# FAVOR attention and a feed-forward block on one core: the attention products of a chunk as one step of eight heads

## The chip, the cores and the metric

The kernel runs on one core of one Trainium2 chip. A core has a matrix engine (TensorE, PE in the profile), VectorE (DVE), ScalarE (ACT), GpSimd (POOL) and SyncE (SP), whose queue here issues the transfers. The engines run their own instruction queues in order and wait for one another by semaphores. The metric is the device time of one execution in microseconds (us), lower is better.

## The reference

Linear attention with positive random features, then a layer norm and a feed-forward block (FFN) with a residual. Batch 8, 8 heads, 576 positions, head width 64, 128 features, model width 512, hidden width 2048.

```python
q_s, k_s = q * scale, k * scale              # scale = 64 ** -0.25
def phi(x):                                  # omega: 128 x 64
    proj = einsum('bhsd,md->bhsm', x, omega)
    h = proj - sum(x * x, -1, keepdims) / 2
    h = h - max(h, -1, keepdims)             # over the 128 features
    return exp(h) / sqrt(128)
q_p, k_p = phi(q_s), phi(k_s)
kv = einsum('bhsm,bhsd->bhmd', k_p, v)
z = sum(k_p, axis=2)
num = einsum('bhsm,bhmd->bhsd', q_p, kv)
den = einsum('bhsm,bhm->bhs', q_p, z)[..., None] + 1e-06
x = (num / den)  as  (8, 576, 512)           # heads side by side
xn = (x - mean) / sqrt(var + 1e-06) * g_ln   # over the 512
out = x + relu(xn @ w_ch1) @ w_ch2
```

## The kernel before, in words

**Tiles.** The 8 x 576 = 4608 tokens are cut into 36 chunks of 128; four chunks make a token tile of 512 (nine tiles, 0 to 8), two chunks a block (18). A chunk can straddle two batches (chunks 4, 13, 22 and 31), and then has its products in two row parts.

**Attention.** The keys of a batch are projected (L510), their row maximum taken (L442, DVE), exponentiated (L448, ACT) and summed with the values into kv (L480), which holds 65 columns a head: 64 of numerator and one of denominator. For a block's queries a transfer (qD) is split into two parts (L573 on ACT, L575 on DVE), projected with two matmuls (L582, L583, a feature pair), copied out of its bank (L230 on ACT), its maximum over the 128 partitions taken by an all-reduce on POOL (L604), subtracted on DVE (L607) and exponentiated (L610, ACT). The names wide0 to wide13 are 14 buffers that all these share.

**A chunk's product** is `gen_x`, the place of the change. PE multiplies query features with kv, one matmul a head and row part (L671), into PSUM banks of four heads each; DVE adds epsilon to the denominators (L678), inverts them (L680) and multiplies (L682) into x; then the layer norm's statistics (L698, L700). `gen_rs` makes the reciprocal root for a block of two chunks at once (L711, ACT at L713 and L715, then L717 to L723 on DVE), so it needs both chunks' statistics. `gen_xnT` normalises a chunk (L741, DVE); PE transposes it (L755, four to a chunk), ACT casts it out of the bank (L759) and DVE makes the low part of the split (L761), both into xnT, the transposed tile.

**FFN.** A token tile has 16 hidden slices. A slice of the first layer (`mm1`, L782 to L784) is 12 matmuls, of three split products for each of four weight parts; its relu is split by ACT and DVE (L793, L795); the second layer (`mm2`, L815 to L817) adds it to four accumulators with 12 matmuls. After the last slice `result` adds x (L826, DVE) and sends the chunk out (L829). The first layer's first slice of the next tile comes behind the second layer's last slice of this one. There is one xnT buffer: the transposes of the next tile can start only when the tile's last first-layer slice is issued, and the first slice needs all four chunks of it.

**What sets the order.** Every step is a Python generator, and a planner runs them all before the kernel exists: a step asks for an engine with an estimated cost, waits for a named event, or gets buffers, and the planner always issues the step that can start first by its estimates, by rank among equals. The FFN's rank is the last, so it fills in where attention has nothing ready. The outcome is one fixed order on each engine. A `get` of one bank is met as soon as any one of its banks is free; a `get` with a count is met only at a moment at which so many are free, and whoever asks for one takes them meanwhile:

```python
count = part.want[2] if len(part.want) > 2 else 1
free = sorted((n for n in what if n in self.places), key=self.places.get)[:count]
if len(free) == count:
```

PSUM has eight banks, b0 to b7. Until the FFN starts, attention has them all; from then on it has b0 and b1 (`at_now()`) for projections, key sums, products and transposes, the first layer b2 and b3, the accumulators b4 to b7. Until the start PE is kept busy with dummy matmuls on b7 (`warm`, L308, called spins here).

Of the kernel before, what the change touches and what calls it, by code (L numbers as in the profile page):

```python
# [17 lines left out]
ALU = mybir.AluOpType  # L18
AX = mybir.AxisListType
PE, ACT, DVE, POOL, SP = "PE", "ACT", "DVE", "POOL", "SP"  # L20
PSUM = bass.MemoryType.PSUM

P = 128
B, H, S, D = 8, 8, 576, 64
M = 128
# [8 lines left out]
EPS = 1e-6  # L34
# [34 lines left out]
class Plan:  # L69
# [73 lines left out]
    def free(self, *names):  # L143
        for n in names:
            assert n not in self.places, n
            self.places[n] = self.cur.seen()
            self.cur.holds -= n[0] == "b" and 0 < self.cur.holds
            self.wake(lambda w: w[0] == "get" and n in w[1])

    def done(self, key):  # L150
        self.made[key] = self.cur.seen()
        self.wake(lambda w: w == ("wait", key))
# [38 lines left out]
def favor_ffn(ctx, tc, kT, kTr, vF, vR, qT, qD, omT, gT, w1, w2, out):  # L191
# [12 lines left out]
    nc = tc.nc  # L204
# [5 lines left out]
    plan = Plan()  # L210
    free, done = plan.free, plan.done
# [7 lines left out]
    def dve(n, k=1, c=0.065):  # L219
        return "run", {DVE: k * (c + 0.00105 * n)}  # L220

    def us(eng, t):
        return "run", {eng: t}
# [16 lines left out]
    def wait(*key):  # L240
        return "wait", key
# [4 lines left out]
    def tile_of(tag, shape, dtype=F32, pool=None):  # L246
        pool = pool or (wp if tag[1].isdigit() and tag[0] == "w" else small if tag[0:2] in ("kv", "mb", "st") or tag[0] == "v" else sb)
        return pool.tile(shape, dtype, tag=tag, name=tag, bufs=1)
# [6 lines left out]
    def bank(tag, n=512):  # L255
        return tile_of(tag, [P, 512], F32, ps)[:, 0:n]
# [10 lines left out]
    mlp_on = []  # L267

    def at_now():
        return b_at if mlp_on else banks  # L270
# [34 lines left out]
    def warm(n):  # L305
        if not mlp_on:
            for _ in range(n):
                nc.tensor.matmul(pw, spin[:, 0:P], spin, start=True, stop=True)  # L308
# [80 lines left out]
    kvs, phis, xs, xnTs, pvs, pvt = {}, {}, {}, {}, {}, {}  # L389
# [27 lines left out]
    def kv_last(b):  # L417
        return kv_key(b, NFULL if b % 2 == 0 else NFULL - 1)
# [195 lines left out]
    def phi(blk, h, cols):  # L614
        p, o = h // 2, h % 2
        s, i = (o, p % 2) if TILED else (p % 2, o)
        return phis[blk, p // 2, s][1][:, i, cols]
# [10 lines left out]
    def gen_block(blk, b_turn):  # L628
        rank = plan.cur.rank
        for j in range(2):  # L630
            if blk < T // QB:
                plan.add(rank, gen_q(blk, j))
            else:
                for s in range(2):
                    plan.add(rank, gen_q2(blk, j, s))
        t_st = yield "get", n_st
        st = tile_of(t_st, [P, 64])
        for i in range(2):
            plan.add(rank + 6 + 2 * i, gen_x(2 * blk + i, t_st, st))
        plan.add(rank + 8, gen_rs(blk, t_st, st))  # L640
        for j in range(2):
            for s in range(2):
                yield wait("phi", blk, j, s)
        yield wait("num", 2 * blk)
        yield wait("num", 2 * blk + 1)
        free(*(phis[blk, j, s][0] for j in range(2) for s in range(2)), b_turn)


    def gen_x(c, t_st, st):
        blk, cols = c // 2, (c % 2) * P  # L650
        ends = sorted({0, P, *(b * S - c * P for b in range(B) if 0 < b * S - c * P < P)})
        parts = [(a, z, (c * P + a) // S) for a, z in zip(ends, ends[1:])]
        for j in range(2):
            for s in range(2):
                yield wait("phi", blk, j, s)
        for _, _, b in parts:
            for s in range(2):
                yield wait(*kv_last(b), s)
        t_x = yield "get", n_x
        x = tile_of(t_x, [P, DM])  # L660
        o = 16 * (c % 2)
        rank = plan.cur.rank

        def half(s):
            t_b = yield "get", at_now()
            yield us(PE, 0.9 * len(parts) if mlp_on else 1.13)
            pn = bank(t_b)[:, 0 : 4 * (D + 1)].rearrange("p (a b) -> p a b", b=D + 1)
            for i in range(4):
                h = 4 * s + i
                for a, z, b in parts:  # L670
                    nc.tensor.matmul(  # L671
                        pn[a:z, i], phi(blk, h, slice(cols + a, cols + z)), kvs[b][1][:, h], start=True, stop=True
                    )
                warm(i % 2)
            done(("nummm", c, s))
            dn = st[:, o + 4 * s : o + 4 * s + 4]
            yield us(DVE, 0.13)
            nc.vector.tensor_scalar(out=dn, in0=pn[:, :, D], scalar1=EPS * M, scalar2=None, op0=ALU.add)  # L678
            yield us(DVE, 0.1)
            nc.vector.reciprocal(dn, dn)  # L680
            yield dve(4 * D, 1, 0.12)
            nc.vector.tensor_tensor(  # L682
                out=x[:, 4 * s * D : 4 * (s + 1) * D].rearrange("p (a b) -> p a b", b=D),
                in0=pn[:, :, 0:D],
                in1=dn.rearrange("p (a b) -> p a b", b=1).to_broadcast([P, 4, D]),
                op=ALU.mult,
            )
            free(t_b)
            done(("x", c, s))

        plan.add(rank, half(0))
        yield from half(1)
        yield wait("nummm", c, 0)
        done(("num", c))
        yield wait("x", c, 0)
        bn, mv = st[:, o + 8 : o + 14], st[:, 32 + 2 * (c % 2) : 34 + 2 * (c % 2)]
        yield dve(DM)
        nc.vector.bn_stats(bn, x)  # L698
        yield us(DVE, 0.1)
        nc.vector.bn_aggr(mv, bn)  # L700
        xs[c] = t_x, x, mv[:, 0:1], st[:, 38 + c % 2 : 39 + c % 2]
        done(("mv", c))
# [224 lines left out]
```

## Time and profile before

| | us |
|---|---|
| median of three runs | 1043.08 |
| lowest, highest | 1042.95, 1043.17 |
| the profiled execution | 1042.56 |
| its span | 1040.8 |
| PE busy | 1032.0 |
| DVE busy | 498.3 |
| ACT busy | 357.1 |
| POOL busy | 133.5 |
| first FFN matmul | 49.07 |

The profile is of one execution. Its rows give the start or the sum of busy time, the mean length of one instruction in ns where a group is shown, and the idle time of the engine just before, with the instruction that ended it. The granted clock of TensorE is 1.0 in the whole run. L12 is line 12 of the kernel before; from L664 on, the lines of the changed kernel have smaller numbers: its product is L670, the reciprocal L682, the statistics of a block L707 to L719, the normalisation L737, the transposes L751, the subtract into xnT L757, the FFN L778 to L780 and L811 to L813, the results L822.

### The profile page before, as it was taken

How to read it: one execution, taken by the hardware profiler on the slowest of the kernel's cores; microseconds unless marked ns; L12 is line 12 of the kernel's file. 1: busy time of each engine (PE TensorE's matmuls, PEld its weight loads, DVE VectorE, ACT ScalarE, POOL GpSimd, SP SyncE). 2: the span in 40 equal slices, each digit the busy share in tenths (PEclk: the TensorE clock that was granted, in tenths of full speed). 3: DMA queues.
4: the chain of work that ended last, by engine and by line, in shares of the span. 5: the costliest groups of instructions: out<-in, count | busy, mean ns of one | idle time of the engine just before them, and what ended most of it. 6: DMA issues, size and time to landing. Idle time of an engine off the chain costs nothing.

```text
span 1040.8 us, 14483 instructions
## 1 busy us (share of the span) xinstructions
PE 1032.0 (99%) x5778; PEld 863.4 (83%) x5778; DVE 498.3 (48%) x1045; ACT 357.1 (34%) x810; POOL 133.5 (13%) x80
## 2 busy tenths in 40 slices
PE   9999999999999999999999999999999999999998
PEld 7888888888887888888887888888878888888886
DVE  6999878366347521663147422751274134113112
ACT  7699746335334421253025421241133111102100
POOL 6000424014002300050002200140022000000000
PEclk9999999999999999999999999999999999999999
DMA  9564222121213100420032100200030010001001
GB/s 358 213 195 150 82 82 91 62 72 51 73 43 130 42 11 1 143 61 1 1 99 85 41 1 1 102 21 1 1 122 1 0 41 1 1 1 42 1 1 41
DMA packets 30308, 64.08 MB, mean 62 GB/s; under 512 B 3488, under 2 KB 3616, under 8 KB 30240
## 3 DMA queue, kind: packets, MB, share of 16 engines
q1 hardware_dynamic: 30240, 63.14, 17.9%
q8 instruction: 46, 0.75, 0.3%
q14 instruction: 22, 0.18, 0.1%
HBM read 53.69 MB, written 9.44 MB: 61 GB/s over the span
## 4 chain that ended last, share of the span: by engine, by line
PE 93%; DVE 4%; DMA 2%; SPq 1%; issue 1%; ACT 0%; ACTq 0%
PE b L815 13%; PE b L782 13%; PE b L784 12%; PE b L817 12%; PE b L816 12%; PE b L783 12%; PE b L480 5%; PE b L671 5%; PE b L510 3%; PE b L582 1%; PE b L583 1%; PE b L755 1%; DMA w<-w 1%; DVE x L826 1%; DMA w<-vF 0%
## 5 line engine op out<-in xcount | busy, mean ns | idle before, releaser
L795 DVE SCALAR_TENSOR_TENSOR hid<-b,hid 128x512 fp32r<-128x512 f32 x144 | 99.3, 689 | 382.5 <-ACT hid L793 381.9
L793 ACT ACTIVATE hid<-b 128x512 fp32r<-128x512 f32 x144 | 86.3, 599 | 445.8 <-PE b L784 445.4
L815 PE MATMUL b<-w,hid 128*128 128x512 f32 x576 | 231.6, 402 | 0.0
L782 PE MATMUL b<-xnT,w 128*128 128x512 f32 x576 | 230.4, 400 | 0.0
L817 PE MATMUL b<-w,hid 128*128 128x512 f32 x576 | 225.2, 391 | 0.0
L784 PE MATMUL b<-xnT,w 128*128 128x512 f32 x576 | 225.0, 391 | 0.1
L816 PE MATMUL b<-w,hid 128*128 128x512 f32 x576 | 224.9, 390 | 0.0
L783 PE MATMUL b<-xnT,w 128*128 128x512 f32 x576 | 224.5, 390 | 0.0
L604 POOL PARTITION_ALL_REDUCE wide<-wide x72 | 132.4, 1877 | 658.2 <-ACT st L713 268.3
L784 PEld LDWEIGHTS b<-xnT,w 128*128 128x128 f32 x576 | 108.2, 188 | 23.6 <-DVE xnT L761 0.5
L817 PEld LDWEIGHTS b<-w,hid 128*128 128x128 f32 x576 | 108.2, 188 | 23.0
L815 PEld LDWEIGHTS b<-w,hid 128*128 128x128 f32 x576 | 108.4, 188 | 22.6
L782 PEld LDWEIGHTS b<-xnT,w 128*128 128x128 f32 x576 | 108.4, 188 | 21.8
L783 PEld LDWEIGHTS b<-xnT,w 128*128 128x128 f32 x576 | 108.4, 188 | 20.6
L816 PEld LDWEIGHTS b<-w,hid 128*128 128x128 f32 x576 | 108.5, 188 | 20.3
L448 ACT ACTIVATE kp<-b,mb 128x128 f32<-128x128 f32 x272 | 75.3, 388 | 51.4 <-DVE mb L442 51.4
L671 PEld LDWEIGHTS b<-kv,wide 128*128 128x128 f32 (+1 forms) x640 | 67.2, 181 | 6.9 <-issue 2.8
L607 DVE TENSOR_TENSOR wide<-wide,wide 128x512 f32<-128x512 f32 x72 | 65.1, 909 | 13.3 <-POOL wide L604 12.8
L480 PEld LDWEIGHTS b<-v,kp 128*128 128x128 f32 (+1 forms) x576 | 64.2, 191 | 6.5 <-issue 1.6
L671 PE MATMUL b<-kv,wide 128*128 128x65 f32 (+1 forms) x640 | 66.8, 261 | 2.3 <-DVE st L678 1.2
L480 PE MATMUL b<-v,kp 128*128 128x65 f32 (+1 forms) x576 | 64.0, 272 | 0.0
L442 DVE TENSOR_REDUCE mb<-b 128x4 f32<-128x512 f32 x72 | 46.6, 681 | 30.9 <-PE b L510 30.8
(71 smaller groups left out, 800.0 us busy)
## 6 DMA issues: line engine op xcount, KB each, us to landing
w<-w SPq DMA_DIRECT2D x32, 512.0 KB, 8.9
wide<-qD SPq DMA_DIRECT2D x64, 256.0 KB, 2.7
out<-x SPq DMA_DIRECT2D x36, 256.0 KB, 2.0
v<-vF SPq DMA_DIRECT2D x28, 260.0 KB, 2.9
wide<-kT SPq DMA_DIRECT2D x28, 256.0 KB, 2.7
w<-vF SPq DMA_DIRECT2D x4, 260.0 KB, 4.8
v<-vR SPq DMA_DIRECT2D x4, 260.0 KB, 4.0
w<-kT SPq DMA_DIRECT2D x4, 256.0 KB, 4.8
```

Of the source, the lines that this page charges most:

```text
L448: nc.scalar.activation(out=kp[:, j], in_=pk[:, i], func=AF.Exp, scale=1.0, bias=mb[:, j : j + 1])
L480: nc.tensor.matmul(o[:, i], kp[r, slot(h)], v[r, h], start=(n > 0 or c + i == 0), stop=(n > 0 or (c == NFULL and i == 3)),)
L604: nc.gpsimd.partition_all_reduce(mx, qc, P, bass_isa.ReduceOp.max)
L671: nc.tensor.matmul(pn[a:z, i], phi(blk, h, slice(cols + a, cols + z)), kvs[b][1][:, h], start=True, stop=True)
L782: nc.tensor.matmul(ph, w[:, 0, cs], xnT[:, 0, k], start=(k == 0), stop=False)
L783: nc.tensor.matmul(ph, w[:, 1, cs], xnT[:, 0, k], start=False, stop=False)
L784: nc.tensor.matmul(ph, w[:, 0, cs], xnT[:, 1, k], start=False, stop=(k == NK - 1))
L793: nc.scalar.activation(out=hl[:, 0], in_=ph, func=AF.Relu)
L795: nc.vector.scalar_tensor_tensor(out=hl[:, 1], in0=ph, scalar=0.0, in1=f32(hl[:, 0]), op0=ALU.max, op1=ALU.subtract)
L815: nc.tensor.matmul(accs[i], hl[:, 0, cs], w[:, 0], start=(f == 0), stop=False)
L816: nc.tensor.matmul(accs[i], hl[:, 0, cs], w[:, 1], start=False, stop=False)
L817: nc.tensor.matmul(accs[i], hl[:, 1, cs], w[:, 0], start=False, stop=(f == NF - 1))
```

## The change

Before, a chunk's product was two generators, one for four heads each; each got one bank, and had its own epsilon, reciprocal and multiplication. Now one step gets two banks at once, issues the matmuls of all eight heads, adds epsilon in two instructions (one for each bank), takes one reciprocal of 128x8 over both, and multiplies in two instructions, after each of which its bank is free. The planner's estimates are the sums of the former ones; the reciprocal's estimate is paid once. The event that says that a chunk's matmuls are issued (`num`) comes now with the step itself.

```diff
-        def half(s):
-            t_b = yield "get", at_now()
-            yield us(PE, 0.9 * len(parts) if mlp_on else 1.13)
-            pn = bank(t_b)[:, 0 : 4 * (D + 1)].rearrange("p (a b) -> p a b", b=D + 1)
-            for i in range(4):
-                h = 4 * s + i
-                for a, z, b in parts:
-                    nc.tensor.matmul(
-                        pn[a:z, i], phi(blk, h, slice(cols + a, cols + z)), kvs[b][1][:, h], start=True, stop=True
-                    )
-                warm(i % 2)
-            done(("nummm", c, s))
-            dn = st[:, o + 4 * s : o + 4 * s + 4]
+        t_b = yield "get", at_now(), 2
+        yield us(PE, 1.8 * len(parts) if mlp_on else 2.26)
+        pn = [bank(t)[:, 0 : 4 * (D + 1)].rearrange("p (a b) -> p a b", b=D + 1) for t in t_b]
+        for h in range(H):
+            for a, z, b in parts:
+                nc.tensor.matmul(
+                    pn[h // 4][a:z, h % 4], phi(blk, h, slice(cols + a, cols + z)), kvs[b][1][:, h], start=True, stop=True
+                )
+            warm(h % 2)
+        done(("num", c))
+        dn = st[:, o : o + H]
+        for s in range(2):
             yield us(DVE, 0.13)
-            nc.vector.tensor_scalar(out=dn, in0=pn[:, :, D], scalar1=EPS * M, scalar2=None, op0=ALU.add)
-            yield us(DVE, 0.1)
-            nc.vector.reciprocal(dn, dn)
+            nc.vector.tensor_scalar(
+                out=dn[:, 4 * s : 4 * s + 4], in0=pn[s][:, :, D], scalar1=EPS * M, scalar2=None, op0=ALU.add
+            )
+        yield us(DVE, 0.1)
+        nc.vector.reciprocal(dn, dn)
+        for s in range(2):
             yield dve(4 * D, 1, 0.12)
             nc.vector.tensor_tensor(
...
-            free(t_b)
-            done(("x", c, s))
-
-        plan.add(rank, half(0))
-        yield from half(1)
-        yield wait("nummm", c, 0)
-        done(("num", c))
-        yield wait("x", c, 0)
+            free(t_b[s])
```

Since the planner sets the order, the change moves far more rows than it edits. Three places follow. In the rows, the left of the arrow is what is written, then what is read; b0 to b7 are banks, x6 and x7 the chunks 6 and 7, st3 the small statistics of their block; the number after an underscore only tells one use of a buffer from another.

PE, the product of chunk 7 in tile 0. Before, its two halves (b0_1706, then b1_1728) are six second-layer matmuls apart, and the next feature pairs (om_hi, om_lo) come behind:

```order
L671 MATMUL b0_1706<-kv1_95,wide5_1583 128x65
...
L815 MATMUL b4_783<-w2_120_1341,hid0_1587 128x512
...
L671 MATMUL b1_1728<-kv1_95,wide11_1489 128x65
...
L815 MATMUL b6_798<-w2_120_1341,hid0_1587 128x512
...
L582 MATMUL b0_1764<-wide4_1680,om_hi_82 128x512
...
L582 MATMUL b1_1776<-wide3_1684,om_hi_82 128x512
```

Now, with 12 first-layer matmuls of slices w1_120 to w1_150 and six second-layer ones between the product of chunk 6 and these rows:

```order
L582 MATMUL b1_1754<-wide4_1680,om_hi_82 128x512
L583 MATMUL b1_1754<-wide4_1680,om_lo_83 128x512
L582 MATMUL b0_1759<-wide3_1687,om_hi_82 128x512
L583 MATMUL b0_1759<-wide3_1687,om_lo_83 128x512
L811 MATMUL b6_795<-w2_130_1373,hid1_1658 128x512
...
L811 MATMUL b7_802<-w2_130_1373,hid1_1658 128x512
...
L670 MATMUL b1_1776<-kv1_95,wide11_1486 128x65
...
L670 MATMUL b0_1777<-kv1_95,wide5_1580 128x65
```

The same two feature pairs now have b1 and b0 ahead of the product of chunk 7, not behind it.

DVE, the statistics of the block of chunks 6 and 7. Before, they follow the product of chunk 7 directly:

```order
L680 RECIPROCAL st3_984<-st3_984 128x4
L682 TENSOR_TENSOR x7_1651<-b1_1728,st3_984 128x256
L698 BN_STATS st3_984<-x7_1651 128x6
L700 BN_AGGR st3_984<-st3_984 128x2
L711 TENSOR_SCALAR st3_984<-st3_984 128x2
L717 TENSOR_TENSOR st3_984<-st3_984 128x2
```

Now they begin behind the third result of tile 0 (b6), and the normalisations (L737) of chunks 6 and 7 are the last rows of this piece:

```order
L822 TENSOR_TENSOR x2_469<-b6_795,x2_469 128x512
L707 TENSOR_SCALAR st3_981<-st3_981 128x2
L822 TENSOR_TENSOR x3_470<-b7_802,x3_470 128x512
L607 TENSOR_TENSOR wide3_1828<-wide3_1828,wide11_1835 128x512
L575 TENSOR_TENSOR wide13_1865<-wide12_1850,wide13_1865 64x512
L607 TENSOR_TENSOR wide1_1884<-wide1_1884,wide10_1890 128x512
L713 TENSOR_TENSOR st3_981<-st3_981 128x2
L442 TENSOR_REDUCE mb0_1457<-b0_1915 128x4
...
L575 TENSOR_TENSOR wide7_1871<-wide6_1862,wide7_1871 64x512
L737 TENSOR_SCALAR wide10_1952<-x6_1638,st3_981 128x512
L607 TENSOR_TENSOR wide9_1905<-wide9_1905,wide0_1929 128x512
L737 TENSOR_SCALAR wide13_1964<-x7_1639,st3_981 128x512
```

The rows left out are three more of the small statistics (L715, L717, L719), a second L442 and an L607.

PE, the change from tile 0 to tile 1. Before, the four chunks are transposed (L755) with 12 second-layer matmuls still to come behind the last of them:

```order
L755 MATMUL b0_1922<-ident_74,wide9_1871 128x128 x4
L815 MATMUL b4_783<-w2_150_1404,hid1_1859 128x512
...
L480 MATMUL b1_1938<-v2_1357,kp1_1459 128x65 x4
L815 MATMUL b7_805<-w2_150_1404,hid1_1859 128x512
...
L782 MATMUL b3_1959<-xnT0_1857,w1_00_368 128x512
```

Now, from behind the last second-layer matmul, two feature pairs and a key projection later:

```order
L582 MATMUL b0_1954<-wide13_1865,om_hi_82 128x512
L583 MATMUL b0_1954<-wide13_1865,om_lo_83 128x512
L480 MATMUL b1_1950<-v2_1354,kp1_1456 128x65 x4
L751 MATMUL b0_1968<-ident_74,wide10_1952 128x128 x4
L480 MATMUL b1_1975<-v2_1354,kp1_1456 128x65 x4
L751 MATMUL b0_1989<-ident_74,wide13_1964 128x128 x4
L582 MATMUL b1_1995<-wide7_1871,om_hi_82 128x512
L583 MATMUL b1_1995<-wide7_1871,om_lo_83 128x512
L778 MATMUL b2_2001<-xnT0_1816,w1_00_368 128x512
```

The transposes of chunks 6 (wide10) and 7 (wide13) stand now between the end of tile 0's second layer and the first matmul of tile 1.

More of the change, by code (lines that the diff above doesn't have):

```diff
@@ L683, in half @@
                 out=x[:, 4 * s * D : 4 * (s + 1) * D].rearrange("p (a b) -> p a b", b=D),
-                in0=pn[:, :, 0:D],
-                in1=dn.rearrange("p (a b) -> p a b", b=1).to_broadcast([P, 4, D]),
+                in0=pn[s][:, :, 0:D],
+                in1=dn[:, 4 * s : 4 * s + 4].rearrange("p (a b) -> p a b", b=1).to_broadcast([P, 4, D]),
                 op=ALU.mult,
             )
-            free(t_b)
-            done(("x", c, s))
-        plan.add(rank, half(0))
-        yield from half(1)
-        yield wait("nummm", c, 0)
-        done(("num", c))
-        yield wait("x", c, 0)
+            free(t_b[s])
         bn, mv = st[:, o + 8 : o + 14], st[:, 32 + 2 * (c % 2) : 34 + 2 * (c % 2)]
```

## Prediction

> **What bounds the kernel now.** I read the page's busy shares first, then the chain of work that ended last.
>
> ```profile
> span 1040.8 us, 14483 instructions
> PE 1032.0 (99%) x5778; PEld 863.4 (83%) x5778; DVE 498.3 (48%) x1045; ACT 357.1 (34%) x810; POOL 133.5 (13%) x80
> PE 93%; DVE 4%; DMA 2%; SPq 1%; issue 1%; ACT 0%; ACTq 0%
> ```
>
> TensorE (PE) sets the end, and 93% of the chain is its own queue. The edit takes no matmul away, so it can only move PE's idle time, and whatever PE gains or loses arrives whole at the end. Next come PE's waits and the cost of the pieces of its stream. A timeline row has the start, the length, the line and the shapes, and in brackets the wait just before it with the instruction that ended the wait; the two rows with "PE b L671" and no shapes are from the chain.
>
> ```profile
> 314.11 0.63 PE L671 MATMUL b<-kv,wide 128*128 128x65 f32 x4 [1.22 <-DVE st L678]
> 547.12 0.63 PE L671 MATMUL b<-kv,wide 128*128 128x65 f32 x4 [1.05 <-DVE st L723]
> 768.51 0.47 PE L582 MATMUL b<-wide,om_hi 128*128 128x512 f32 x1 [1.05 <-DVE st L678]
> 141.14 1.73 PE b L671 x16
> 144.32 0.84 PE b L671 x8
> 49.85 0.50 PE L784 MATMUL b<-xnT,w 128*128 128x512 f32 x1
> ```
>
> Once the FFN runs, three rows have a wait of 1 us or more, 3.3 us together, all at products of chunks that straddle two batches (13, 22, 31). A block of 8 products (half a chunk) takes 0.84, one of 16 takes 1.73: one step of 16 instead of two of 8 buys PE nothing. The last row is the FFN's third matmul, late for the fourth transposed chunk.
>
> The remaining place where PE could stop is a change of token tile. There is one buffer for the transposed tile (xnT), freed by the last first-layer matmul of a tile, so the transposes of the next must hide under what is left of the second layer. The first such change, before:
>
> ```profile
> 162.51 0.60 PE L755 MATMUL b<-ident,wide 128*128 128x128 f32 x4
> 165.04 1.00 PE L480 MATMUL b<-v,kp 128*128 128x65 f32 x8
> 165.84 0.48 PE L815 MATMUL b<-w,hid 128*128 128x512 f32 x1
> 166.16 0.39 PE L816 MATMUL b<-w,hid 128*128 128x512 f32 x1
> 166.39 0.40 PE L817 MATMUL b<-w,hid 128*128 128x512 f32 x1
> 166.62 0.40 PE L782 MATMUL b<-xnT,w 128*128 128x512 f32 x1
> 167.08 0.39 PE L784 MATMUL b<-xnT,w 128*128 128x512 f32 x1
> 165.84 0.68 DVE L761 TENSOR_TENSOR xnT<-b,xnT 128x512 fp32r<-128x512 f32 x1
> ```
>
> The last subtract of xnT (L761) ends at 166.52 and its reader, the third matmul, starts at 167.08: hidden, with 0.56 us to spare. Spacing inside the stream is 0.23 (166.16 to 166.39), and 0.32 for the first matmul after another kind of work (165.84 to 166.16).
>
> **The change part by part.** VectorE (DVE) loses one reciprocal per chunk:
>
> ```profile
> L680 DVE RECIPROCAL st<-st 128x4 f32<-128x4 f32 x72 | 12.2, 173 | 1.0
> L678 DVE TENSOR_SCALAR st<-b 128x4 f32<-128x4 f32 x72 | 10.9, 154 | 11.8 <-PE b L671 11.1
> L682 DVE TENSOR_TENSOR x<-b,st 128x256 f32<-128x256 f32 x72 | 30.0, 421 | 1.1
> ```
>
> 36 fewer of 0.17 is 6.2 us of DVE, an engine with half the span idle; a reciprocal of 8 columns instead of 4 I take as equal (bounds: 0.13 to 0.35, twice the row). FFN matmuls cover this saving nearly everywhere, so it counts only where PE waits for DVE.
>
> A, the first tile change. The product of chunk 7 now needs both banks at one moment. In the new order the query features take the single banks as they come free, and between the step of chunk 6 and that of chunk 7 stand 12 first-layer and 12 second-layer matmuls and two feature pairs (L582, L583): 28 x 0.23 = 6.4 us on PE. A product whose second half began at 144.3 (the chain's row of 8) begins near 151. What follows it on DVE then no longer fits ahead of the end of tile 0. The reciprocal root of chunks 6 and 7 (now L707 to L719) stands on DVE behind three additions of tile 0's results (now L822), which cannot start before the second layer's last block ends on PE, and the two normalisations (now L737) stand behind that. On PE the transposes of 6 and 7 come after the last second-layer matmul of tile 0: nothing is left to hide them. Durations for that chain:
>
> ```profile
> L607 DVE TENSOR_TENSOR wide<-wide,wide 128x512 f32<-128x512 f32 x72 | 65.1, 909 | 13.3 <-POOL wide L604 12.8
> L575 DVE TENSOR_TENSOR wide<-wide,wide 64x512 fp32r<-64x512 f32 x64 | 50.3, 788 | 11.9 <-ACT wide L573 10.4
> L442 DVE TENSOR_REDUCE mb<-b 128x4 f32<-128x512 f32 x72 | 46.6, 681 | 30.9 <-PE b L510 30.8
> L826 DVE TENSOR_TENSOR x<-b,x 128x512 f32<-128x512 f32 x36 | 23.5, 684 | 6.5 <-PE b L817 6.3
> L741 DVE TENSOR_SCALAR wide<-x,st 128x512 f32<-128x512 f32 x36 | 18.6, 539 | 0.1
> L717 DVE TENSOR_TENSOR st<-st 128x2 f32<-128x2 f32 x18 | 4.3, 241 | 6.0 <-ACT st L715 6.0
> L761 DVE TENSOR_TENSOR xnT<-b,xnT 128x512 fp32r<-128x512 f32 x36 | 23.9, 685 | 7.7 <-ACT xnT L759 7.7
> L759 ACT CAST xnT<-b 128x512 fp32r<-128x512 f32 x36 | 20.2, 587 | 20.8 <-PE b L755 20.8
> 151.53 1.16 PE L510 MATMUL b<-om,wide 64*128 64x128 f32 x16
> ```
>
> When would PE want the fourth chunk? Before tile 1's first matmul the new order has 16 feature pairs instead of 11 and otherwise the same matmuls: 5 x 2 x 0.23 = 2.3 later, less 0.3 (start) and some 0.8 for fewer blocks in between (D), so 166.6 becomes 167.9 and the third matmul 168.4. Between tile 0's last matmul and this first one lie four feature pairs (1.8), one key projection (1.16), key sums (8, 1.0) and two transposes (0.8): 4.8. So tile 0 ends at 163.1; its third result is added by then, and L707 is through at about 163.1. Behind L707, in the order of the rows: the fourth result 0.68, four L607 3.64, two L575 1.58, two maxima 1.36, four statistics of about 0.2 to 0.25, 0.9, two normalisations 1.08: 9.2, so the seventh chunk is normalised at 172.3. Then the subtract of chunk 6 (0.69, whose bank chunk 7's transposes take), transposes 0.35, cast 0.59, subtract 0.69: 174.6. Four L607 also wait for GpSimd (POOL), and small operations are slowed beside it:
>
> ```profile
> 148.25 0.17 DVE L711 TENSOR_SCALAR st<-st 128x2 f32<-128x2 f32 x1
> 149.43 0.85 DVE L717 TENSOR_TENSOR st<-st 128x2 f32<-128x2 f32 x1 [1.01 <-ACT st L715]
> 168.66 8.84 POOL L604 PARTITION_ALL_REDUCE wide<-wide  x5 [6.92 <-ACT wide L230]
> 170.47 1.53 DVE L607 TENSOR_TENSOR wide<-wide,wide 128x512 f32<-128x512 f32 x1 [1.76 <-POOL wide L604]
> ```
>
> 0.85 against 0.17 for a 128x2 operation; I add 0.8 for such. 175.4 less 168.4: **A = +7.0**. Low bound: every row at its undisturbed length (L607 0.68, small ones 0.16, starting 0.5 earlier) and PE 0.4 later, +4. High bound: each of the four L607 as long as that 1.53 row instead of the mean of 0.91, 2.5 more, and 0.5 for the other SBUF operations, +10. While PE stands there, its attention work has already been done, so none of it fills the hole.
>
> [...] The quoted row, the longest L607, has 1.53, and the mean is 0.91, so the trace shows a slowing, not whole blocking. [...]
>
> B, the three stalls, 3.3 us. In the new order chunk 13's step has both banks well in time: -1.2. At chunk 22 the statistics of the block before are still on DVE ahead of the bank's release, about 1.0 of its 1.05 stays. At chunk 31, L607 waits for POOL and some 0.35 stays. Sum 3.3 to 1.35: **B = -2.0** (-3.3 with all gone, 0 with none).
>
> C, the start.
>
> ```profile
> 49.12 0.68 DVE L761 TENSOR_TENSOR xnT<-b,xnT 128x512 fp32r<-128x512 f32 x1
> 25.00:50.00 25.00, 24.48 (x229) 21.42 (x228) 24.86 (x73) 15.65 (x34) 1.75 (x3) 1.00 0.59 233
> ```
>
> DVE (third column of busy time) works 24.86 of those 25 us, and the FFN's third matmul waits for its last subtract: the one place where DVE time is the kernel's time. Four reciprocals fewer is -0.7, but a pair of banks is waited for where one was enough. **C = -0.3** (-0.7 to +0.2).
>
> D: other blocks that interrupt the FFN stream fall by some ten (36 blocks of L671 become 32, key sums 47 to 41). At 0.09 each that is -0.9; other pieces (24 key sums at once) may give some back. **D = -0.5** (-1.4 to 0).
>
> Nothing on the page speaks for the DMA queues or the weights as a cost: the out transfers are moved among the key loads on SP's queue, which are due many us later. One spin (a dummy matmul of the start) is added, under 0.2 us.
>
> Sum: +7.0 - 2.0 - 0.3 - 0.5 = **+4.2**. The profiled execution took 1042.56, 1.8 more than its span and 0.5 less than the median of 1043.08; so profiled about 1046.8, median about **1047.3**.
>
> **The rivals.**
>
> Short chain (0.20). A at its low end: 4 - 2.8 = +1.2, 1044.3. For it: PE's work ahead could be longer than counted, and DVE rows beside an idle POOL are short. Against: the L607 there each wait for an all-reduce.
>
> Hidden, faster (0.08). The normalisations are ready when PE wants them, and only the gains are left: -2.8, 1040.3. It decides at chunk 7's normalisation: ready by 166 there is no stall; up to 168.8 the gains still outweigh it. For it: before, the same work came in time, with 0.56 to spare. Against: the order puts 14 rows of DVE between L707 and it, 7.2 us even at their shortest, and L707 waits for the end of tile 0.
>
> Lock (0.03). [...]
>
> Banks run dry (0.02). Every product holds both attention banks, and PE waits each time for a division, 32 chunks after the start at about 0.5 (L678 twice and the reciprocal): +16, 1059. [...] Against: the new order puts 2.5 us or more of FFN matmuls between a product and the next user of its banks.
>
> **How the numbers follow.** The forecast has the remaining 0.67. Its own range, A from 4 to 10, is 1044.3 to 1050.3. The range for 8 in 10 reaches a little into the short chain with B at its best, 1043.6, and ends at 1050.3; outside lie the faster case, the lock, the dry banks and some of the tails. A measurement of this kernel can tell about 0.2% (2.1 us) from no change. Faster by more: the hidden case, 0.08. Within: the short chain, 0.20. Slower: forecast, lock and dry banks, 0.72.
>
> **What would show it.** Right: one gap of 4 to 10 us on PE ahead of tile 1's third matmul near 168 to 176, with DVE's last xnT subtract as its releaser, DVE full over that stretch, no wait at chunk 13, and later tile changes as before. Wrong: no such gap (hidden), a gap of under 4 (chain over-counted), many gaps of half a microsecond at products (dry banks), L607 rows of 2.4 (lock), or a second tile change that stalls as well.

## The result and the profile after

The changed kernel takes 1049.88 us (median of 4, 1049.44 to 1050.41) against 1043.01 us for the kernel before (4 runs beside it): a ratio of 1.0065, 95% interval 1.0054 to 1.0077. It is 6.9 us slower; the forecast was 4.2 us slower, 1047.3, with 1050.3 as the upper end of its range.

The page of the changed kernel, its span, its busy shares and the granted clock in 40 slices:

```profile
span 1047.6 us, 14445 instructions
PE 1036.2 (99%) x5779; PEld 866.0 (83%) x5779; DVE 493.5 (47%) x1008; ACT 357.2 (34%) x811; POOL 135.5 (13%) x80
PEclk9999998999999999999999999999999999999999
```

DVE has 4.8 us less to do, as the edit says, and the kernel is slower all the same. PE's busy time is 4.2 us longer for the same work, and one slice of the clock, the one from 157 to 183 us, is not at full speed. The waits of PE, with their sum, number and longest:

```profile
PE b L582 <- ACT kp L448: 3.6, 1, 3.6
PE b L582 <- DVE x L685: 1.7, 2, 1.0
PE b L308 <- DVE spin L274: 1.2, 1, 1.2
```

The last of these is the start of the program. The first is new, the second is what is left of the three waits before. The first change of token tile on PE's timeline:

```profile
162.23 0.39 PE L813 MATMUL b<-w,hid 128*128 128x512 f32 x1
...
163.75 1.64 PE L510 MATMUL b<-om,wide 64*128 64x128 f32 x16 [0.22 <-ACT wide L230]
168.97 0.80 PE L582 MATMUL b<-wide,om_hi 128*128 128x512 f32 x1 [3.58 <-ACT kp L448]
169.56 0.63 PE L583 MATMUL b<-wide,om_lo 128*128 128x512 f32 x1
170.13 1.97 PE L480 MATMUL b<-v,kp 128*128 128x65 f32 x8
171.90 1.06 PE L751 MATMUL b<-ident,wide 128*128 128x128 f32 x4
172.75 1.80 PE L480 MATMUL b<-v,kp 128*128 128x65 f32 x8
174.36 1.12 PE L751 MATMUL b<-ident,wide 128*128 128x128 f32 x4
...
176.15 0.50 PE L778 MATMUL b<-xnT,w 128*128 128x512 f32 x1 [0.20 <-ACT xnT L755]
...
176.88 0.49 PE L780 MATMUL b<-xnT,w 128*128 128x512 f32 x1
```

The second layer of tile 0 ends at 162.6, and the third matmul of tile 1 (L780) starts at 176.88; before, these were 166.8 and 167.08. In between PE stands idle for 3.6 us in front of a feature pair, and afterwards its rows are nearly twice as long as usual: eight key sums (L480) take 1.97 and 1.80, not 1.00. The windows of that stretch give the granted clock beside PE's busy time:

```profile
155.00:164.00 9.00, 8.78 (x44) 1.00 0.39 126
164.00:169.00 5.00, 1.42 (x17) 0.96 0.58 195
169.00:172.00 3.00, 3.00 (x11) 0.50 0.00 0
172.00:177.00 5.00, 4.80 (x22) 0.66 0.11 21
177.00:185.00 8.00, 8.00 (x56) 1.00 0.25 88
```

The clock falls to 0.50 at about 168.6, near the end of the wait (0.96 on average from 164 to 169), and is back at 1.00 from about 175.4 (0.66 on average from 172 to 177). What the feature pair waited for is two steps away, as DVE's timeline and one row of ACT show:

```profile
162.80 0.92 DVE L707 TENSOR_SCALAR st<-st 128x2 f32<-128x2 f32 x1
...
165.65 1.42 DVE L607 TENSOR_TENSOR wide<-wide,wide 128x512 f32<-128x512 f32 x1
...
168.23 0.68 DVE L442 TENSOR_REDUCE mb<-b 128x4 f32<-128x512 f32 x1
...
171.46 1.26 DVE L737 TENSOR_SCALAR wide<-x,st 128x512 f32<-128x512 f32 x1
...
176.13 0.69 DVE L757 TENSOR_TENSOR xnT<-b,xnT 128x512 fp32r<-128x512 f32 x1 [1.21 <-ACT xnT L755]
```

```profile
167.78 2.30 ACT L448 ACTIVATE kp<-b,mb 128x128 f32<-128x128 f32 x8
```

The maxima (L442) stand in the chain behind L707; the exponentials (L448) wait for them, and four of them hold each bank until they are done; the feature pair wants the first of these banks. Chunk 7 is normalised at 172.72 and its last subtract begins at 176.13.

Where the loss stands, from the timelines: the time from tile 0's third matmul (49.85 before, 49.88 now) to the same matmul of a later tile.

| up to the third matmul of | before | now | difference |
|---|---|---|---|
| tile 1 | 117.23 | 127.00 | +9.77 |
| tile 2 | 259.53 | 267.15 | +7.62 |
| tile 3 | 376.48 | 382.88 | +6.40 |
| tile 5 | 605.68 | 612.29 | +6.61 |
| tile 8 | 900.44 | 906.80 | +6.36 |

The five feature pairs put ahead of tile 1 are given back within that tile (9.77 to 7.62), the wait behind chunk 13's product is gone in tile 2 (7.62 to 6.40), and after that hardly anything moves.

### The profile page after: what moved, and what is told of

The parts are those of the page before. It is cut to its first block, busy times and chain, and to the rows that moved or that the text cites. A ratio compares the mean times of both kernels' runs of the same rounds, so it can differ in the third digit from the quotient of the medians.

```text
span 1047.6 us, 14445 instructions
## 1 busy us (share of the span) xinstructions
PE 1036.2 (99%) x5779; PEld 866.0 (83%) x5779; DVE 493.5 (47%) x1008; ACT 357.2 (34%) x811; POOL 135.5 (13%) x80
## 4 chain that ended last, share of the span: by engine, by line
PE 92%; DVE 5%; DMA 1%; issue 1%; ACT 0%; SPq 0%
PE b L778 13%; PE b L811 13%; PE b L780 12%; PE b L779 12%; PE b L813 12%; PE b L812 12%; PE b L480 5%; PE b L670 5%; PE b L510 3%; PE b L582 1%; PE b L751 1%; PE b L583 1%; DVE wide L607 1%; DMA w<-w 1%; DVE wide L575 0%
## 5 line engine op out<-in xcount | busy, mean ns | idle before, releaser
L780 PE MATMUL b<-xnT,w 128*128 128x512 f32 x576 | 224.9, 390 | 0.1
L780 PEld LDWEIGHTS b<-xnT,w 128*128 128x128 f32 x576 | 108.1, 188 | 23.9 <-DVE xnT L757 0.9
L448 ACT ACTIVATE kp<-b,mb 128x128 f32<-128x128 f32 x272 | 75.0, 388 | 64.3 <-DVE mb L442 64.2
L607 DVE TENSOR_TENSOR wide<-wide,wide 128x512 f32<-128x512 f32 x72 | 62.9, 875 | 19.8 <-POOL wide L604 19.3
L480 PEld LDWEIGHTS b<-v,kp 128*128 128x128 f32 (+1 forms) x576 | 64.8, 194 | 6.2 <-issue 2.0
L442 DVE TENSOR_REDUCE mb<-b 128x4 f32<-128x512 f32 x72 | 46.8, 684 | 43.5 <-PE b L510 43.5
L480 PE MATMUL b<-v,kp 128*128 128x65 f32 (+1 forms) x576 | 65.0, 277 | 0.0
```

The lines of the kernel that those rows point to most:

```text
L448: nc.scalar.activation(out=kp[:, j], in_=pk[:, i], func=AF.Exp, scale=1.0, bias=mb[:, j : j + 1])
L480: nc.tensor.matmul(o[:, i], kp[r, slot(h)], v[r, h], start=(n > 0 or c + i == 0), stop=(n > 0 or (c == NFULL and i == 3)),)
L780: nc.tensor.matmul(ph, w[:, 0, cs], xnT[:, 1, k], start=False, stop=(k == NK - 1))
```

## The experiments

All were timed beside runs of the kernel before, whose median was 1042.95 to 1043.06 each time. The start moves from run to run (VectorE's first maximum began between 6.27 and 7.60 in the profiles). The last column therefore gives the profiled time from the first FFN matmul to the end of the last one, against 987.97 before.

| run | median, us | ratio (95%) | FFN, against before |
|---|---|---|---|
| changed kernel | 1049.88 | 1.0065 (1.0054 to 1.0077) | +6.4 |
| same order, two reciprocals | 1050.14 | 1.0068 (1.0056 to 1.0081) | +7.0 |
| dummy matmuls in the wait | 1048.47 | 1.0052 (1.0039 to 1.0064) | +5.0 |
| step from chunk 16 | 1043.82 | 1.0007 (0.9998 to 1.0016) | -0.1 |
| reciprocal alone | 1040.54 | 0.9976 (0.9966 to 0.9985) | -3.0 |
| pairs reserved | 1052.63 | 1.0096 (1.0082 to 1.0110) | +8.4 |
| step from chunk 8 | 1044.70 | 1.0021 (1.0012 to 1.0031) | +0.8 |
| step for chunk 7 alone | 1045.01 | 1.0026 (1.0017 to 1.0035) | +1.5 |
| reciprocal alone's order, two reciprocals | 1040.81 | 0.9981 (0.9973 to 0.9990) | -2.9 |
| step for chunks 13, 22, 31 | 1039.91 | 0.9972 (0.9961 to 0.9982) | -3.7 |

**The reciprocal in the changed order.**

```diff
         yield us(DVE, 0.1)
-        nc.vector.reciprocal(dn, dn)
+        for s in range(2): nc.vector.reciprocal(dn[:, 4 * s : 4 * s + 4], dn[:, 4 * s : 4 * s + 4])
```

> The changed kernel with its order on every engine kept, but 36 x one reciprocal of 8 columns put back as two of 4. Theory (a reciprocal is covered by the FFN's matmuls everywhere but at the start): between 0 and +0.7 us against the changed kernel, 1049.9 to 1050.6. Rival (VectorE's time counts everywhere): 36 x 0.17 = +6, about 1056.

1050.14, 0.26 more than the changed kernel, and the two intervals overlap. The 36 reciprocals are worth next to nothing: VectorE's saving is covered, and the loss is in the order. The 0.6 more in the last column is not VectorE's alone, since in this profile the clock stayed at 0.50 for 10.2 us (167.9 to 178.1), not 6.8.

**The clock in the wait.** 36 dummy matmuls fill the 3.58 us:

```diff
+        if (blk, j, s) == (5, 1, 0):
+            pad = tile_of("b3", [P, 512], F32, ps)[:, 0 : 2 * P]
+            for _ in range(36):
+                nc.tensor.matmul(pad, spin[:, 0:P], spin, start=True, stop=True)
         pq = bank(t_b)
         nc.tensor.matmul(pq, om_hi, qs, start=True, stop=False)
```

> The changed kernel with 36 dummy matmuls of 0.11 us (3.9 us) on PE inside the stall at the first tile change, between the key projection and the feature pair that waits 3.58 us for ScalarE; they write a bank that nothing uses there. Theory (part of the stall is the clock, 0.50 and 0.66 in the 8 us after PE's idle time): the clock stays at 1.0, the rows behind it take their usual time (8 key sums 0.8 instead of 1.8), and 1.6 us come back: about 1048.3. Rival (the rows behind wait for VectorE anyway): 1049.9, clock or not. If the matmuls run longer than the wait: slower by what is over, under 0.5.

1048.47, 1.4 less. Windows and timeline of this run (lines are 4 larger from there on):

```profile
164.00:169.00 5.00, 4.86 (x46) 1.00 0.62 196
169.00:172.00 3.00, 2.75 (x22) 1.00 0.15 58
172.00:177.00 5.00, 4.23 (x31) 1.00 0.28 87
...
165.72 4.10 PE L584 MATMUL b<-spin 128*128 128x256 bf16 x36
169.58 0.48 PE L586 MATMUL b<-wide,om_hi 128*128 128x512 f32 x1
...
170.54 1.11 PE L480 MATMUL b<-v,kp 128*128 128x65 f32 x8 [0.25 <-ACT kp L448]
```

The clock stays at 1.00, the key sums take 1.11, and 1.4 us come back, each of its five executions (1048.01 to 1048.96) under each of the changed kernel's four: that part of the loss is the clock. The rest stays, because chunk 7 is no earlier on VectorE: it is normalised at 173.12 in this run, whose FFN began 0.4 later, against 172.72. Counted from the first FFN matmul, tile 1 began after 125.6, against 127.05 in the changed kernel.

**The loss is one event.**

```diff
+        if c < 16:
+            (the two halves, each with one bank, as before)
+        else:
             (the step with two banks)
```

> Chunks 0 to 15 as before in two halves, one step with two banks from chunk 16 on. Theory (the loss is one event, the first tile change): no wait there, the transposes of chunks 6 and 7 ahead of the last second-layer block as before, and chunk 13 waits 1.2 as before: 1042.9, from 1042.0 to 1043.5. Rival (each step with two banks costs a little): 20 of 36 steps keep 20/36 of +6.9, about 1046.8.

1043.82, no difference that can be told, a little above the expected range: its FFN took as long as before, 987.9, and its start 1.0 longer. The 20 later steps cost nothing that can be told; the rival's 3.8 us are absent. So the loss needs the steps of chunks 0 to 15. PE's waits:

```profile
PE b L582 <- DVE x L719: 1.7, 2, 1.0
PE b L673 <- DVE st L680: 1.2, 1, 1.2
```

The wait behind chunk 13's product (1.2, L673) is there; the two at 22 and 31 are those of the changed kernel (1.7).

**The reciprocal alone.**

```diff
         def half(s):
             t_b = yield "get", at_now()
...
-            yield us(DVE, 0.1)
-            nc.vector.reciprocal(dn, dn)
+            done(("den", c, s))
+            if s:
+                yield wait("den", c, 0)
+                yield us(DVE, 0.1)
+                nc.vector.reciprocal(st[:, o : o + H], st[:, o : o + H])
+                done(("rec", c))
+            else:
+                yield wait("rec", c)
```

> The reciprocal alone: two halves with a bank each as before, got one by one, but one reciprocal of 8 columns for both (the first half holds its bank until the second's denominators are there). Theory (the loss is from asking for two banks at once): no late transposes at any tile change, 1042.7, from 1041.5 to 1043.5. Rival (the shared reciprocal delays the first half's bank): waits of half a microsecond at products, 1045 or more.

1040.54: better than the kernel before, and better than expected (its FFN part is 3.0 shorter). PE's waits:

```profile
PE b L308 <- DVE spin L274: 1.2, 1, 1.2
PE b L762 <- DVE wide L748: 0.5, 1, 0.5
PE b L672 <- DVE x L689: 0.2, 1, 0.2
```

The three waits of 3.3 us have shrunk to 0.2. Whether the shorter VectorE or the other order did that, a later run tells.

**Is chunk 7's step starved?**

```diff
+            rival = any(p.want[0] == "get" and len(p.want) > 2 and p.key < part.key and set(p.want[1]) & set(what)
+                        for p in self.blocked if p is not part)
-            if len(free) == count:
+            if len(free) == count and not (count == 1 and rival):
```

> The changed kernel with one rule more in the planner: a single bank is not given to a step of lower priority while a step of higher priority waits for two. Theory A (the step for chunk 7 is starved by requests for single banks, and that alone makes the loss): the product comes earlier, the wait at the first tile change goes, 1042 to 1044. Theory B (any step that needs both of only two banks makes everything else in the chain wait, whoever goes first): in this order chunk 7's product stands behind all 384 FFN matmuls of tile 0 (348 in the changed kernel, 318 before), so product, statistics, root, normalisation, transposes and split lie bare: a wait of 9 us or more instead of 7.6, 1051 to 1055.

1052.63, within theory B's range. The FFN's time is 8.4 longer than before. The wait of 9 us or more is not there as one piece: the three waits shown come to 4.6, and the clock is at 0.50 from about 167.3 to 181.0. PE's timeline at the tile change, and two of its windows:

```profile
163.59 1.97 PE L672 MATMUL b<-kv,wide 128*128 128x65 f32 x16 [1.47 <-DVE xnT L759]
166.60 1.28 PE L482 MATMUL b<-v,kp 128*128 128x65 f32 x8 [1.04 <-DVE x L687]
167.81 2.61 PE L512 MATMUL b<-om,wide 64*128 64x128 f32 x16
172.55 2.17 PE L753 MATMUL b<-ident,wide 128*128 128x128 f32 x8 [2.13 <-ACT kp L450]
...
170.00:175.00 5.00, 2.58 (x10) 0.50 0.43 121
175.00:180.00 5.00, 4.93 (x20) 0.50 0.12 45
```

With priority for pairs the product of chunk 7 (L672, x16) is not earlier but behind the tile's last FFN matmul. Protecting the request does not mend it. A reading that no run separates: with two banks for everything, a pair held by one step is two banks that no feature pair has, and the features of the next products are late instead.

**Where the step begins.**

```diff
+        if c < 8:
+            (the two halves, as before)
```

> Chunks 0 to 7 in two halves as before, one step with two banks from chunk 8 on. Theory (whichever tile change is planned with the transposes behind the last second-layer matmul loses; not the start): no wait at the first tile change, but one at the second, where two transposes and 12 key sums stand between the last matmul of tile 1 and the first of tile 2: 2 to 8 us on PE there, 1045 to 1050. Rival (only the first change is tight on VectorE): no wait at the second, 1042 to 1044.

1044.70, just under the expected range: the wait at the first tile change is gone, and one appears at the second, smaller than expected. PE's timeline there:

```profile
306.16 0.63 PE L785 MATMUL b<-ident,wide 128*128 128x128 f32 x4 [0.57 <-DVE xnT L791]
306.99 3.19 PE L480 MATMUL b<-v,kp 128*128 128x65 f32 x24 [0.20 <-DVE xnT L791]
```

With one ahead of the first transpose these are three gaps of 0.2 to 0.6; up to tile 2's third matmul this kernel has lost 1.1 us. The transposes stand behind the second layer, as expected, but their inputs are nearly there. Late transposes alone were cheap in this execution; in the changed kernel the chain on VectorE is late with them. The median hides a spread: eight of the ten executions took 1043.7 to 1045.1 with a mean granted clock of 0.999 or more, two took 1047.4 and 1047.9 with 0.997. An estimate from these means: 0.003 of some 1045 us is 3 us, or 6 us at 0.50. In those two the gaps seem to have cost the clock as well; no profile here shows them.

**Chunk 7 alone.**

```diff
+        if c != 7:
+            (the two halves, as before)
```

> One step with two banks for chunk 7 alone. Theory A (chunk 7's starved step is enough): most of the loss, 1046 or more. Theory B (it takes the delays of the steps before it too): in this order its product stands at 324 of tile 0's 384 FFN matmuls and the last transposes at 372 as before, so no wait of more than 0.5 us at the first tile change, 1042 to 1044.

1045.01: between the two theories, and neither holds: there is a wait of 2.2 us, though the transposes stand where they did. PE's timeline, two rows of DVE's, and the windows around the wait:

```profile
169.88 0.47 PE L582 MATMUL b<-wide,om_hi 128*128 128x512 f32 x1 [2.19 <-DVE xnT L791]
...
166.65 2.49 DVE L856 TENSOR_TENSOR x<-b,x 128x512 f32<-128x512 f32 x4
169.05 1.28 DVE L791 TENSOR_TENSOR xnT<-b,xnT 128x512 fp32r<-128x512 f32 x2
...
166.00:170.00 4.00, 1.81 (x9) 1.00 0.63 235
170.00:173.00 3.00, 3.00 (x18) 1.00 0.29 109
```

The last two subtracts into xnT stand behind all four results of tile 0, and a feature pair waits for the bank that they hold. One step of this kind, at one chunk, loses 2.2 us by tile 2's third matmul (261.7 against 259.5); the other 5.4 of the 7.6 come with the steps of other chunks, 1.4 of them by the clock. The wait of 2.2 us did not move the clock in this execution. Of the ten, seven took 1044.6 to 1045.3 with a mean granted clock of 1.000, and three 1047.3 to 1047.5 with 0.998: there, it seems, the same order did lose the clock (no profile shows them), and those three reach theory A's 1046. Which execution was profiled decides what this wait appears to cost.

**What the reciprocal alone gains from.**

```diff
-                nc.vector.reciprocal(st[:, o : o + H], st[:, o : o + H])
+                for r in range(0, H, 4): nc.vector.reciprocal(st[:, o + r : o + r + 4], st[:, o + r : o + r + 4])
```

> The kernel with the reciprocal alone (1040.54), its order kept on every engine, but each reciprocal of 8 columns put back as two of 4. Theory A (its gain of 2.4 is the order that the planner arrives at, in which the three waits of chunks 13, 22 and 31 have gone): 1040.5 to 1041.2. Theory B (the gain is VectorE's time): back to 1042.5 or more.

1040.81: theory A. With all 72 reciprocals back in that order the gain stays; what changed the time was the order that the planner arrives at when the product's estimates and the time for which it holds its banks are a little different.

**The step where two banks help.**

```diff
+        if c not in (13, 22, 31):
+            (the two halves, as before)
```

> One step with two banks only for chunks 13, 22 and 31, the three that straddle two batches and whose products wait 3.3 us in the kernel before; all others in two halves. Theory (the step takes the wait at chunk 13 away, and leaves at 22 and 31 what it leaves in the changed kernel, 0.98 and 0.71, with no cost at a tile change): 1.5 us faster, about 1041.5. Rival (the waits come from chains on VectorE that the step doesn't shorten): 1043.

1039.91, the lowest median of all, 3.0 us under the kernel before. PE's waits, and the product of chunk 22:

```profile
PE b L308 <- DVE spin L274: 1.2, 1, 1.2
PE b L785 <- DVE wide L771: 0.4, 1, 0.4
...
548.31 1.15 PE L704 MATMUL b<-kv,wide 128*64 128x65 f32 x32
```

All three waits are gone, more than expected: what the changed kernel has left at 22 and 31 is not the step of these chunks, but comes with the steps around them. The shapes also say where the waits stood. The product of a chunk that straddles is 128x64 in its rows, and chunk 22's stood in one block of 32 before, too (at 544.92, without a wait). The row that waited 1.05 us behind it, at 547.12, is 128x128: the first half of chunk 23's product. In this run a 128x128 product, by the count chunk 23's, stands ahead of chunk 22's, at 544.38 and without a wait, so the gain is here again a matter of order.

## Why the prediction was right, and where its terms were off

**What bounds it.** Right in the main: PE's time carries the whole difference, and 4.8 us less on VectorE bought nothing (the run with the same order). But the text let only PE's idle time move; PE's speed, which it had at nothing, moved too.

**A, the first tile change, +7.0 forecast, +7.6 measured** by tile 2. The mechanism is the one forecast. Chunk 7's product began at 150.6 (151 forecast), L707 was through at 163.7 (163.1 forecast), chunk 7 normalised at 172.7 (172.3, and 0.8 more for POOL).

The size is in part luck, for two errors cancel. The first is a step that is missing from the sum, the clock. Behind the normalisation the text allowed 2.3 us to the last subtract's end; it took 4.1, to 176.8, with PE's rows at a clock of 0.50, and 2.7 in the run in which the wait was filled and the clock stayed at 1.00. That run shows that 1.4 us of the 7.6 are the clock. The second goes the other way: between tile 0's last matmul and tile 1's first the text counts eight key sums (1.0 us), but the rows of the change show two groups of four heads there, which are 16 in the profile. With them tile 0's end would have been forecast 1.0 earlier, at 162.1 (measured 162.6), and A at 6.0; with the clock's 1.4 that is 7.4.

The place and the look of the stall were also not as forecast. PE idled in front of a feature pair, released by exponentials (L448), for a bank that the same VectorE chain held, and the longest gap was 3.58 us, not 4 to 10. By the text's own list a gap under 4 meant that the chain was over-counted. It was not: from L707's end to chunk 7's normalisation it took 9.0 us, against 9.2 and 0.8 for POOL. The gap was shorter because two feature pairs, 16 key sums and two groups of transposes were still to come behind it, where the text had all of that done before PE stands still. The other signs held: VectorE was busy for 3.94 of each 4 us from 164 to 172, the wait at chunk 13 went, and no later tile change stalls.

The longest single wait does not settle what the clock did in these runs. Within the 3.58 us here it fell to 0.50 (at 168.6), behind 2.2 us, in the profiled execution with the step for chunk 7 alone, it stayed at 1.00, and in the run with reserved banks it was 0.50 from 167.3, behind waits of 1.5 and 1.0 us. Nor does the work that follows: here it began again at 168.97, and the clock was at 1.00 6.4 us later; in the run with the same order and two reciprocals it took some 9.5 us (about 168.7, by its windows, to 178.1).

**B, -2.0 forecast, -1.6 measured** by the waits. The 1.2 at chunk 13 went, as forecast (7.62 to 6.40). At chunk 22 the wait became 0.98, as forecast, and at 31 it is 0.71 where 0.35 was forecast. The text puts the three waits at the products of chunks 13, 22 and 31; its own rows have 128x128 shapes and a feature pair, so they stood at the work behind those products. That much of the waits at 22 and 31 stays belongs to this order: with the step at three chunks alone all three went.

**C, -0.3 forecast, -0.1 at most measured.** The third matmul starts 43.4 us after VectorE's first maximum before (49.85 less 6.46) and 43.3 now (49.88 less 6.59). The shift of the start from run to run is larger than the term.

**D, -0.5 forecast, not seen.** What is left of 6.36 after A (7.62) and B (-1.6) is +0.4, not -0.5; what D did within tiles 0 and 1 is in A's 7.62. The span adds 0.5 behind the last matmul. So the sum missed by 2.7: 0.6 in A, 0.4 in B, 0.3 in C, 0.9 in D and 0.5 at the end, all of them small and all on one side.

**The rivals.** Hidden and short chain are out: the chain was as long as counted. Dry banks is out: after the start and outside of tile 0's end PE's only waits of half a microsecond or more are the two of 22 and 31. Lock is out: no run shows the L607 rows of 2.4 that the list of signs gives for it. The longest in that stretch took 1.42; in both kernels the longest of all took 1.53, beside an all-reduce, and those beside an idle POOL 0.69 at most. The cause given for the late step, single requests that starve it, is not all of it: reserving the banks made it worse, and chunk 7's step alone costs 2.2 of 7.6 in the profiled execution. What the runs support is that a step that needs both of the two banks can make the whole chain of tile 1 later, whoever goes first; how the 5.4 us divide over the other chunks was not measured, nor why the steps from chunk 16 on cost nothing. The edit also merges the planner's estimates and moves the event `num`; no run separates these from the two banks.

## What to carry to other kernels

Asking for two buffers at once out of a pool of two is another thing than asking twice for one: look at who else lives from that pool, and give the pair only where a run shows that it helps, as here at three chunks of 36. When a scheduler sets the order, an edit of a few tenths of a microsecond is priced by the order it leads to, and not by its own instructions: one kernel here gained 2.2 us with all 72 reciprocals in it, another 3.0 us with three of them saved. And where a stall of several microseconds on the matrix engine is forecast, add the slow rows behind it (here 1.4 of 7.6 us, behind a wait of 3.58), and look at the single executions and their clock, since a median can hide that some of them had less of it (two of ten, at a mean of 0.997, in one run here, and three of ten, at 0.998, in another).

## What was not expected of the hardware

Near the end of an idle time of 3.58 us TensorE's granted clock fell to 0.50, for 6.8 us, nearly all of it filled with work (168.6 to 175.4); in the run with the same order and two reciprocals, in whose windows PE stands idle for 3.8 us in all from 163 to 172, it was 0.50 for 10.2 us. So the same order of work did not get the clock back after the same time. In the run with reserved banks two shorter waits, 1.5 and 1.0 us within five, were followed by 0.50 as well, for 13.7 us with a further wait in them. The three lengths, 6.8, 10.2 and 13.7, are very nearly as two to three to four. After a wait of 2.2 us the clock was 1.00 in the profiled execution with the step for chunk 7 alone. A reciprocal of 128x8 took 0.20 us on average against 0.17 for 128x4.
